# Attention, experts and MLP in one kernel on one core: another order for its first part

## The chip, the cores and the metric

The kernel runs on one core of a Trainium2 chip. The metric is the device time of one execution in microseconds (us). The time before is the median of three runs.

## The reference

What is computed, cut to what matters (B, H, S, D = 2, 8, 576, 64; 1152 tokens; all in float32):

```
scores = q @ k^T / sqrt(D) + cum[i] - cum[j]      # cum: running sum of log(clip(f, 1e-4, 1)); causal
attn   = softmax(scores);  x = attn @ v           # x: 1152 tokens x 512
p      = domain_probs / (domain_probs.sum(-1) + 1e-9)
y      = sum over 4 experts e of p[:, e] * (relu(x @ w1[e]) @ w2[e])     # 512 -> 1024 -> 512
out    = (h * sigmoid(1.702 h)) @ w_out,  h = y @ w_in                   # 512 -> 2048 -> 512
```

## The kernel before

**Tiles.** Tokens are the free dimension, in four chunks: chunk 0 is batch 0, tokens 0 to 255; chunk 1 batch 0, 256 to 575; chunks 2 and 3 the same of batch 1. Later, three wide chunks of 384 are used. Attention goes by units. A unit of chunk 0 (a "plain" unit) is one head and two tiles of 128 queries; a later unit is a pair of heads and one tile of 128 queries (64 of both heads in the last). A unit passes the stages of `STAGES` (L538): scores on TensorE into one of two `s` banks (L427), their maximum on VectorE (`mx`, L453), `exp` on ScalarE (L467), division by the sum on GpSimd (L478), transposes on TensorE (L497), one or two rounds of work later the product with the values (`x`, L527), and x split into a rounded part xh and a rest xl (L535).

**Split operands.** Weights and later keys and queries are written as a rounded part and a rest (`whi`, `wlo`; `khi`, `klo`; `qhi`, `qlo`), and a product is three matmuls instead of one. Weights come by DMA into four buffers `wst` of two groups each (`load_pair`), `whi` is made on ScalarE or GpSimd and `wlo` on VectorE (`split_w`, `split_rest`, L171). Keys and queries of a pair are split on GpSimd (`prep_parts`, `prep_queries`, L357 to L366), which also adds the causal mask to rows of `cum` broadcast from DRAM (`prep_cum`, `cb` and `cbs`, L379 to L388). Plain units take unsplit operands that were laid out on the host.

**Layers.** The experts and the MLP are cut into 12 blocks of 512 hidden columns (`NBLK`); a visit of a block computes its first layer (L619) for its chunks and its second layer (L663) for them, each as four groups g of 12 matmuls. Visit 0 is block 2 (expert 1) of chunk 0. Its first layer is not done at once but grows as heads of chunk 0 come out (`emit_first`, L640). `seq` (L126) is the order of layers: first layer of visit 0, first of visit 1, second of visit 0, first of visit 2, second of visit 1, and so on. The second layer's result is multiplied by the probabilities, broadcast over partitions as `dpb0` and `dpb1` (L674, L677), and summed in `acc`. `dpb0` and `dpb1` first hold the values of chunk 0, heads 0 to 3 and 4 to 7 (L310), and are loaded with probabilities of experts 0 and 1 from the DRAM tile `dpT` when those have been read (L776, L777); `dpT` is written from `dpn`, which `make_probabilities` makes on GpSimd and VectorE (L262 to L273). `ps_m` gives three banks for the layers' sums.

**Order.** All is written in program order in `attention()` (L545), one `yield` per unit, and in the main loop (L783), which pulls units between the layers' groups at a pace set by `due`. A scheduler then sets the order on each engine, except where `keep_in_program_order` pins an instruction. In the first loop (L761) each pull of chunk 0 is followed by dummy matmuls (`turn`, L712: `WARM` of them at the very start, then those of `FILL`) and, at pulls 4 to 7, by the split of the first weights `wa`. The preparation of a later pair of heads is made `LEAD` = 3 units ahead of its first unit; for the first pair that falls into chunk 0, behind the normalisation of one of its units (`pinned`, L561). The weights `wb` of visit 0 are split in the main loop, at the first group (L801).

## Time and profile before

| | us |
|---|---|
| median of 3 runs (lowest, highest) | 743.79 (742.61, 744.67) |
| the profiled execution, its own time | 741.27 |
| its span from first to last instruction | 739.6 |
| TensorE matmul busy (share of the span) | 717.7 (97%) |
| VectorE busy | 454.9 (62%) |
| GpSimd busy | 294.2 (40%) |
| ScalarE busy | 271.5 (37%) |
| mean granted clock of TensorE | 0.988 of 2.4 GHz |

The span lies inside the execution's own time. Matmuls are pipelined and overlap, so busy TensorE is not TensorE at its peak. PE is TensorE, DVE VectorE, ACT ScalarE, POOL GpSimd, SP SyncE, which issues most DMAs; an L number is a line of the kernel.

### The profile page before, as it was taken

The page shows a single profiled execution, that of the slowest core. Times are in us where ns is not written, and L with a number is a line of the kernel's source. Part 1 is how long each engine was busy: PE and PEld are TensorE (multiplying, and loading weights), DVE is VectorE, ACT ScalarE, POOL GpSimd, SP SyncE. Part 2 cuts the span into 40 slices and gives each one's busy share as a digit, 9 for nine tenths or more (in the row PEclk, how much of TensorE's full clock was granted, in tenths as well). Part 3 has the DMA queues.
Part 4 walks back from the last instruction along what each step waited for, and adds up shares of the span by engine and source line. Part 5 has one row for each costly group of instructions (what it writes and reads, how often), then busy time and mean ns, then how long its engine had stood idle before and what let it go on. Part 6 is the DMA issues. An engine that isn't in the chain of part 4 may idle for free.

```text
span 739.6 us, 12033 instructions
## 1 busy us (share of the span) xinstructions
PE 717.7 (97%) x4516; PEld 683.9 (92%) x4518; DVE 454.9 (62%) x1024; ACT 271.5 (37%) x634; POOL 294.2 (40%) x372
## 2 busy tenths in 40 slices
PE   7969799999999999999999999999999999999998
PEld 4757599899999999999999999999999999999997
DVE  4756455667757999999899733344973134334422
ACT  4565454556641233222212221222444433323420
POOL 3898776785333004223232433332452222222220
PEclk9998899999999999999999999999999999999999
DMA  8765643523216354553343301000100000000012
GB/s 285 241 191 168 207 157 101 168 81 97 75 48 226 132 188 158 174 177 121 120 145 105 102 2 56 1 1 1 58 0 1 1 1 1 1 1 0 1 43 86
DMA packets 31226, 68.83 MB, mean 93 GB/s; under 512 B 3224, under 2 KB 4768, under 8 KB 31168
## 3 DMA queue, kind: packets, MB, share of 16 engines
q1 hardware_dynamic: 31128, 68.02, 29.1%
q8 instruction: 36, 0.59, 0.3%
q14 instruction: 22, 0.18, 0.1%
q10 hardware_dynamic: 40, 0.04, 0.0%
HBM read 65.62 MB, written 2.41 MB: 92 GB/s over the span
## 4 chain that ended last, share of the span: by engine, by line
PE 88%; DMA 6%; DVE 5%; issue 1%; ACT 1%; SPq 0%; ACTq 0%; DVEq 0%
PE m L663 38%; PE m L619 37%; PE s L427 4%; PE x L527 4%; PE t L497 3%; DMA wst<-in_wa_moe_dram 1%; DVE wlo L171 1%; DMA mst<-in_wa_mlp_dram 1%; DMA dpT<-dpn 1%; DMA dpb<-dpT 1%; PE m L640 1%; DVE cvd L234 1%; PE m L712 1%; DMA kd<-fr 1%; DVE cvt L220 1%
## 5 line engine op out<-in xcount | busy, mean ns | idle before, releaser
L679 POOL TENSOR_TENSOR acc<-acc,tmp 128x384 f32<-128x384 f32 (+3 forms) x112 | 114.1, 1030 | 238.1 <-DVE tmp L677 237.7
L663 PE MATMUL m<-hh,whi 128*128 128x384 f32 (+2 forms) x640 | 128.7, 321 | 4.9 <-DVE acc L674 4.9
L663 PE MATMUL m<-hl,whi 128*128 128x384 f32 (+2 forms) x640 | 128.7, 320 | 0.0
L663 PE MATMUL m<-hh,wlo 128*128 128x384 f32 (+2 forms) x640 | 127.8, 320 | 0.8 <-DVE wlo L171 0.7
L619 PE MATMUL m<-xh,whi 128*128 128x384 f32 (+2 forms) x624 | 126.2, 322 | 0.0
L619 PE MATMUL m<-xh,wlo 128*128 128x384 f32 (+2 forms) x624 | 125.6, 321 | 0.0
L619 PE MATMUL m<-xl,whi 128*128 128x384 f32 (+2 forms) x624 | 124.7, 320 | 0.0
L56 ACT ACTIVATE whi<-wst 128x512 fp32r<-128x512 f32 x108 | 67.7, 631 | 126.6 <-PE m L619 72.2
L663 PEld LDWEIGHTS m<-hh,whi 128*128 128x128 f32 x640 | 106.1, 189 | 6.7 <-DVE acc L674 5.1
L663 PEld LDWEIGHTS m<-hh,wlo 128*128 128x128 f32 x640 | 106.2, 189 | 1.5 <-DVE wlo L171 1.4
L663 PEld LDWEIGHTS m<-hl,whi 128*128 128x128 f32 x640 | 106.8, 189 | 0.3
L619 PEld LDWEIGHTS m<-xh,whi 128*128 128x128 f32 x624 | 104.1, 189 | 0.6 <-DVE wlo L171 0.4
L619 PEld LDWEIGHTS m<-xh,wlo 128*128 128x128 f32 x624 | 104.2, 189 | 0.1
L619 PEld LDWEIGHTS m<-xl,whi 128*128 128x128 f32 x624 | 103.9, 189 | 0.1
L171 DVE TENSOR_TENSOR wlo<-wst,whi 128x512 fp32r<-128x512 f32 x112 | 89.8, 807 | 20.1 <-ACT whi L56 16.4
L654 POOL TENSOR_TENSOR hl<-tmp,hh 128x384 fp32r<-128x384 f32 x48 | 49.1, 1025 | 133.4 <-ACT hh L56 133.3
L645 ACT ACTIVATE hh<-m 128x384 fp32r<-128x384 f32 (+2 forms) x112 | 49.0, 438 | 117.6 <-PE m L619 117.2
L646 DVE SCALAR_TENSOR_TENSOR hl<-m,hh 128x384 fp32r<-128x384 f32 (+2 forms) x112 | 54.9, 495 | 34.6 <-ACT hh L645 34.4
L677 DVE TENSOR_TENSOR tmp<-m,dpb 128x384 f32<-128x384 f32 (+2 forms) x80 | 41.0, 513 | 31.8 <-PE m L663 28.5
L652 DVE TENSOR_TENSOR tmp<-m,sg 128x384 f32<-128x384 f32 x48 | 26.6, 554 | 54.2 <-ACT sg L651 54.2
L478 POOL TENSOR_SCALAR e<-e,sm 128x128 f32<-128x128 f32 (+4 forms) x72 | 47.1, 665 | 31.9 <-DVE sm L476 25.3
L467 ACT ACTIVATE e<-e,mx 128x128 f32<-128x128 f32 (+4 forms) x72 | 42.0, 584 | 33.1 <-DVE mx L453 28.2
(96 smaller groups left out, 772.5 us busy)
## 6 DMA issues: line engine op xcount, KB each, us to landing
wst<-in_wa_moe_dram SPq DMA_DIRECT2D x28, 512.0 KB, 4.1
wst<-in_wb_moe_dram SPq DMA_DIRECT2D x28, 512.0 KB, 3.7
mst<-in_wa_mlp_dram SPq DMA_DIRECT2D x16, 512.0 KB, 3.5
mst<-in_wb_mlp_dram SPq DMA_DIRECT2D x16, 512.0 KB, 4.6
cb<-cumd SPq DMA_DIRECT2D x16, 256.0 KB, 6.7
qr<-in_qk_dram SPq DMA_DIRECT2D x12, 256.0 KB, 6.8
kq<-in_qk_dram SPq DMA_DIRECT2D x8, 352.0 KB, 13.1
vd<-in_vp_dram SPq DMA_DIRECT2D x8, 320.0 KB, 4.4
```

The source lines that it names most:

```text
L56: return nc.scalar.activation(out=out, in_=in_, func=AF.Copy)
L171: sub = nc.vector.tensor_sub(lf, raw, f(hf))
L427: nc.tensor.matmul(pt[:, :z - a], lhsT=lr[i][0], rhs=lr[i][1], start=i == 0, stop=i == n - 1)
L467: nc.scalar.activation(out=e[:, off:off + w], in_=e[:, off:off + w], func=AF.Exp, scale=-1.0, bias=mx, accum_out=sm[:, 0, k:k + 1])
L478: last_norm[:] = [nc.gpsimd.tensor_scalar(out=e[:, off:off + w], in0=e[:, off:off + w], scalar1=sm[:, 0, i:i + 1], scalar2=1.0, op0=ALU.mu ...
L619: nc.tensor.matmul(p[:, :n], lhsT=w[:, k, :], rhs=x[c][:, k, :], start=(j == 0 and k == 0), stop=(j == 2 and k == 3))
L645: nc.scalar.activation(out=hh[:, g, :n], in_=p[:, :n], func=AF.Relu)
L646: nc.vector.scalar_tensor_tensor(out=hl[:, g, :n], in0=p[:, :n], scalar=0.0, in1=f(hh[:, g, :n]), op0=ALU.max, op1=ALU.subtract)
L654: nc.gpsimd.tensor_sub(hl[:, g, :n], t[:, :n], f(hh[:, g, :n]))
L663: nc.tensor.matmul(p[:, :n], lhsT=w[:, k, :], rhs=x[:, k, :n], start=(j == 0 and k == 0), stop=(j == 2 and k == 3))
L677: nc.vector.tensor_mul(t[:, :n], p[:, :n], d)
L679: nc.gpsimd.tensor_add(a, a, t[:, z])
```

## The change

- `make_probabilities` runs on VectorE and early, its input is loaded among the first DMAs, and `dpT` is written right behind the first four pairs of weights.
- Every load of the first part goes through `load`, which pins its place on SP's queue. Keys and queries of the first later pair come before the plain operands of heads 4 to 7 and before weights; the broadcasts of `cum` are loaded apart from the mask additions (`load_cum`).
- `prep_parts` and `prep_queries` of that first pair stand ahead of the first unit of chunk 0, and its maxima are pinned on VectorE. An empty unit is put in behind the plain units.
- `wa` of visit 0 is split at pulls 2 to 5, `wb` at pulls 7 to 10, with its rounded part on GpSimd.
- `seq` has the second layer of visit 0 right behind its first layer, and the last first-layer sum is evacuated at once.
- 14 dummy matmuls at the start instead of 12, 17 between the units instead of 18.

```diff
-WARM, FILL = 12, (4, 4, 3, 2, 1, 1, 1, 1, 1)
+WARM, FILL = 14, (4, 4, 3, 2, 1, 1, 1, 1)
+    def load(out, in_):
+        ins = nc.sync.dma_start(out=out, in_=in_)
+        if start[0]:
+            tc.keep_in_program_order(ins)
...
-    seq = [(1,) + units[0]]
-    for p_, u in zip(units, units[1:]):
+    seq = [(1,) + units[0], (2,) + units[0], (1,) + units[1]]
+    for p_, u in zip(units[1:], units[2:]):
...
+        hi_ins = (round_pool if v_ == 0 and kind == "b" or 0 < v_ <= 2 and g == 3 else round_act)(hf, raw)
...
-            if v_ == 0 and kind == "a":
+            if v_ == 0:
                 tc.keep_in_program_order(sub)
...
-        nc.gpsimd.tensor_add(s, v[:, 0], v[:, 1])
+        tc.keep_in_program_order(nc.vector.tensor_add(s, v[:, 0], v[:, 1]))
...
-        nc.gpsimd.tensor_mul(out, v, s.unsqueeze(1).to_broadcast([128, 4, NT // 128]))
-        nc.sync.dma_start(out=dpT.rearrange("e (p j) -> p e j", p=128), in_=out)
+        nc.vector.tensor_mul(out, v, s.unsqueeze(1).to_broadcast([128, 4, NT // 128]))
+        return out
...
+                if (c, u) == first_later:
+                    tc.keep_in_program_order(ins)
...
+    unit_seq.insert(max(i for i, (c, u) in enumerate(unit_seq) if plain(c)) + 1, (None, ((), ())))
...
+        prep_parts(*nxt[0])
+        prep_queries(*nxt[0], nxt[0][0][0][0])
...
+            if i == 0:
+                load_cum(*nxt[0])
+            if i == 4:
+                load_heads(*nxt[1])
...
     load_plain(0)
+    dp_raw = load_probabilities()
     load_plain(4)
...
             load_plain_rest(4)
+            load_heads(passes[1], 0, True)
             load_plain_late()
...
-    for _ in range(2):
-        load_pair(True)
-    load_heads(passes[1], 0)
+    dpn = make_probabilities(dp_raw)
+    for _ in range(4):
+        load_pair()
+    load(dpT.rearrange("e (p j) -> p e j", p=128), dpn)
+    load_values(passes[1], 0)
...
-        if pulled[0] in (4, 5, 6, 7):
-            split_w("a", 0, pulled[0] - 4)
-            split_rest()
+        for kind, p0 in (("a", 2), ("b", 7)):
+            if 0 <= pulled[0] - p0 < 4:
+                split_w(kind, 0, pulled[0] - p0)
+                split_rest()
...
-            if i == 0 and g == 0:
-                for k in range(4):
-                    split_w("b", 0, k)
+            if i == 0 and g == 3:
+                evac[0]()
+                evac[0] = lambda: None
```

The scheduler moves more than these lines say; three places in its order follow.

GpSimd, around the split of the first later pair (`kq` its keys, `qr` its queries; each pair of `e` rows is the normalisation of one unit of chunk 0, of which five stand ahead of this piece). Before:

```order
L478 TENSOR_SCALAR e<-e,sm 128x256
L53 TENSOR_SCALAR khi<-kq 128x704
L53 TENSOR_SCALAR qhi<-qr 128x256 x2
L357 TENSOR_TENSOR klo<-kq,khi 128x704
L366 TENSOR_TENSOR qlo<-qr,qhi 128x256 x2
L478 TENSOR_SCALAR e<-e,sm 128x128
```

With the change, from the last row of the setup on:

```order
L53 TENSOR_SCALAR tri<-ones 128x128
L53 TENSOR_SCALAR khi<-kq 128x704
L53 TENSOR_SCALAR qhi<-qr 128x256
L363 TENSOR_TENSOR klo<-kq,khi 128x704
L53 TENSOR_SCALAR qhi<-qr 128x256
L372 TENSOR_TENSOR qlo<-qr,qhi 128x256 x2
L491 TENSOR_SCALAR e<-e,sm 128x128
L491 TENSOR_SCALAR e<-e,sm 128x256
```

The split has moved from behind the fifth unit's normalisation to ahead of the first unit's.

TensorE, from the second pair's first scores on (L619 is a first layer, here that of visit 1). Before:

```order
L427 MATMUL s<-khi,qhi 128x384
L427 MATMUL s<-khi,qlo 128x384 x2
L427 MATMUL s<-klo,qhi 128x384 x2
L497 MATMUL t<-identr,e 128x128 x3
L619 MATMUL m<-xh,whi 128x256 x4
L497 MATMUL t<-identr,e 128x128 x3
```

With the change (L683 is the second layer, here of visit 0, and L639 the first):

```order
L683 MATMUL m<-hh,whi 128x256 x6
L683 MATMUL m<-hh,wlo 128x256 x4
L683 MATMUL m<-hl,whi 128x256 x3
L683 MATMUL m<-hh,whi 128x256
L683 MATMUL m<-hh,wlo 128x256 x4
L683 MATMUL m<-hl,whi 128x256 x5
L683 MATMUL m<-hh,whi 128x256 x4
L510 MATMUL t<-identr,e 128x128 x3
```

Behind the same scores now stand 27 matmuls of the second layer, and then the first transposes `t` of chunk 1 (pair 0, unit 0), where before they stood at once. Ahead of the last transposes of chunk 1 (pair 3, its third unit) the whole order has 235 matmuls of layers other than `emit_first`, where before it had 176.

SP's queue, around the two loads of broadcast probabilities (`dpb_76` is `dpb0`, `dpb_77` is `dpb1`). Before, with 46 rows ahead of the write of `dpT`:

```order
L273 DMA dpT<-dpn 128x4x9
L146 DMA wst<-in_wb_moe_dram 128x2x512
L385 DMA cbs<-cumd 128x1x576
L776 DMA dpb_76<-dpT 128x576
L777 DMA dpb_77<-dpT 128x576
```

With the change, where that write has 12 rows ahead of it:

```order
L796 DMA dpb_76<-dpT 128x576
L62 DMA wst<-in_wb_moe_dram 128x2x512
L62 DMA cb<-cumd 128x512 x2
L62 DMA cbs<-cumd 128x1x576
L62 DMA kq<-in_qk_dram 128x704
L62 DMA qr<-in_qk_dram 128x512
L62 DMA vd<-in_vp_dram 128x640
L797 DMA dpb_77<-dpT 128x576
```

`dpb1`, which the second layer of visit 0 needs first, is now loaded behind the rows of the second and third pair of chunk 1, in row 29 of the queue instead of row 51.

## Rows read from the trace of the kernel before

**Rows 1.** Page: TensorE's busy tenths and granted clock, 40 slices of the span.

```profile
PE   7969799999999999999999999999999999999998
PEclk9998899999999999999999999999999999999999
```

**Rows 2.** Windows: stretch and length; busy us by engine; PEclk; DMA share; GB/s.

```profile
0.00:9.10 9.10, 5.10 (x12) 1.67 (x13) 3.82 (x7) 3.60 (x5) 3.87 (x11) 1.00 0.74 175
9.10:27.86 18.76, 18.70 (x104) 12.89 (x106) 13.31 (x57) 11.78 (x43) 11.03 (x18) 0.91 0.88 320
27.86:66.50 38.64, 30.22 (x174) 22.09 (x174) 23.72 (x70) 19.69 (x53) 36.37 (x64) 0.91 0.65 202
66.50:100.00 33.50, 28.27 (x190) 24.54 (x189) 16.60 (x57) 16.78 (x45) 25.20 (x36) 0.90 0.53 159
100.00:739.60 639.60, 635.36 (x4044) 622.75 (x4043) 397.49 (x834) 219.63 (x491) 217.72 (x246) 1.00 0.24 75
```

**Rows 3.** Waits of TensorE: us in total, times, longest.

```profile
PE m L663 <- DVE acc L674: 4.9, 1, 4.9
PE s L427 <- DVE mx L453: 3.5, 2, 2.5
PE t L497 <- POOL e L478: 2.4, 3, 1.3
PE s L427 <- POOL qlo L366: 1.9, 1, 1.9
```

**Rows 4.** Timeline, TensorE: start, us, instruction, [idle before, releaser].

```profile
1.85 5.10 PE L712 MATMUL m<-acc 128*128 128x512 bf16 x12 [1.85 <-DVE acc L705]
...
27.86 0.51 PE L427 MATMUL s<-khi,qhi 128*128 128x384 f32 x2
...
50.16 0.64 PE L619 MATMUL m<-xh,wlo 128*128 128x256 f32 x4
50.64 0.64 PE L619 MATMUL m<-xl,whi 128*128 128x256 f32 x4
...
110.36 0.71 PE L497 MATMUL t<-identr,e 128*128 128x128 f32 x5
```

**Rows 5.** Timeline, GpSimd, in the same columns.

```profile
12.55 0.83 POOL L478 TENSOR_SCALAR e<-e,sm 128x128 f32<-128x128 f32 x2 [7.99 <-DVE sm L476]
...
16.67 1.26 POOL L478 TENSOR_SCALAR e<-e,sm 128x128 f32<-128x128 f32 x2 [0.98 <-ACT ph L56]
...
22.24 0.77 POOL L53 TENSOR_SCALAR khi<-kq 128x704 fp32r<-128x704 f32 x1
...
27.24 2.46 POOL L478 TENSOR_SCALAR e<-e,sm 128x128 f32<-128x128 f32 x6
...
41.38 3.05 POOL L478 TENSOR_SCALAR e<-e,sm 128x384 f32<-128x384 f32 x2
...
56.86 0.62 POOL L53 TENSOR_SCALAR whi<-wst 128x512 fp32r<-128x512 f32 x1
57.46 1.15 POOL L478 TENSOR_SCALAR e<-e,sm 128x384 f32<-128x384 f32 x2
```

**Rows 6.** Windows, GpSimd alone: all of a stretch; then instructions on `dps` alone.

```profile
29.67:105.40 75.73, 65.16 (x101) 0.91 0.60 185
...
40.00:80.00 40.00, 2.05 (x5) 0.91 0.62 187
```

**Rows 7.** Timeline, VectorE, in the columns of rows 4.

```profile
16.85 0.73 DVE L171 TENSOR_TENSOR wlo<-wst,whi 128x512 fp32r<-128x512 f32 x1
...
30.00 0.41 DVE L453 CUSTOM_DVE_ANT_0 e<-s,cb 128x256 f32<-128x256 f32 x1
...
39.77 4.28 DVE L171 TENSOR_TENSOR wlo<-wst,whi 128x512 fp32r<-128x512 f32 x5 [0.17 <-ACT whi L56]
```

**Rows 8.** Chain of waits that ended last: start, us, what.

```profile
4.49 4.48 DMA kd<-fr
...
75.43 6.76 DMA dpT<-dpn
82.60 6.65 DMA dpb<-dpT
```

More of the change, by code (lines that the diff above doesn't have):

```diff
@@ L145, in load_pair @@
             t = wst_p.tile([128, 2, 512], F32, tag="wst", name="wst")
[L146 to L148 removed]
+            load(t, (wa_moe if kind == "a" else wb_moe)[b, g:g + 2].rearrange("g p c -> p g c"))
             raw_w[kind, v_, g] = t[:, 0, :]
@@ L171, in rest @@
             sub = nc.vector.tensor_sub(lf, raw, f(hf))
-            if v_ == 0 and kind == "a":
+            if v_ == 0:
                 tc.keep_in_program_order(sub)
@@ L258, in load_probabilities @@
         raw = const.tile([128, NT // 32], F32, name="dpraw")
-        nc.sync.dma_start(out=raw, in_=dp)
+        load(raw, dp)
         return raw
@@ L310, in load_plain @@
         vd = (dpb1 if h0 else dpb0)[:, :2 * G * D].rearrange("p (t g d) -> p t g d", t=2, g=G)
-        for i, t in enumerate((kd, qd)):
-            if h0 == 0 or i == 0:
-                nc.sync.dma_start(out=t[0:64], in_=qk0[h0 // G, i].rearrange("d (g s) -> d g s", g=G))
+        if h0 == 0:
+            for i, t in enumerate((kd, qd)):
+                load(t[0:64], qk0[0, i].rearrange("d (g s) -> d g s", g=G))
         nc.gpsimd.memset(qd[64:65], 1.0 / NEG)
@@ L321, in load_plain_rest @@
         if h0 == 0:
-            tc.keep_in_program_order(nc.sync.dma_start(out=kd[64:65], in_=cum[h0:h0 + G, :wk]))
+            load(kd[64:65], cum[h0:h0 + G, :wk])
         else:
@@ L343, in load_heads, with load_values @@
         st["kq"] = kq_p.tile([128, KW], F32, tag="kq", name="kq")
-        nc.sync.dma_start(out=st["kq"], in_=src[:, :KW])
+        load(st["kq"], src[:, :KW])
         for i, c in enumerate(cs):
             st["q", c] = kq_p.tile([128, QW], F32, tag="qr", name="qr")
-            nc.sync.dma_start(out=st["q", c], in_=src[:, KW + i * QW:KW + i * QW + QW])
+            load(st["q", c], src[:, KW + i * QW:KW + i * QW + QW])
+        if not later:
+            load_values(p, h0)
+    def load_values(p, h0):
+        cs, b, s0 = p
+        st = pairs[p, h0]
         st["vd"] = v_p.tile([128, 5, 2, D], F32, tag="vd", name="vd")
-        nc.sync.dma_start(out=st["vd"], in_=vp[b * H // 2 + h0 // 2].rearrange("p (t g d) -> p t g d", t=5, g=2))
+        load(st["vd"], vp[b * H // 2 + h0 // 2].rearrange("p (t g d) -> p t g d", t=5, g=2))
     def prep_parts(p, h0):
@@ L366, in prep_queries, with load_cum @@
             nc.gpsimd.tensor_sub(lo[:, a:a + 256], raw[:, a:a + 256], f(hi[:, a:a + 256]))
+    def load_cum(p, h0):
+        cs, b, s0 = p
+        st = pairs[p, h0]
+        r = b * H + h0
+        st["cb"] = [cb_p.tile([128, 896], F32, tag="cb", name="cb") for _ in range(2)]
+        for g, cb in enumerate(st["cb"]):
+            load(cb[:, :512], cumd[r + g:r + g + 1, :512].to_broadcast([128, 512]))
+        st["cbs"] = cbs_p.tile([128, S], F32, tag="cbs", name="cbs")
+        load(st["cbs"], cumd[r:r + 2, :].unsqueeze(1).to_broadcast([2, 64, S]))
     def prep_cum(p, h0):
@@ L371, in prep_cum @@
         st = pairs[p, h0]
-        r = b * H + h0
-        st["cb"] = []
-        for g in range(2):
-            cb = cb_p.tile([128, 896], F32, tag="cb", name="cb")
-            nc.sync.dma_start(out=cb[:, :512], in_=cumd[r + g:r + g + 1, :512].to_broadcast([128, 512]))
+        for cb in st["cb"]:
             nb = (384 - s0) // 128
@@ L428, in emit_scores @@
         raw_s[c, u] = out
+    first_later = units_of(1, 0)[0]
     def emit_max(c, u):
@@ L566, in attention, with prepare @@
             done = None
-            new = [k for k in nxt if first[k] == i + LEAD]
-            new_q = [k for k, j in first_q.items() if j == i + LEAD]
-            if i > n0:
+            new = [k for k in nxt if first[k] == i + LEAD and k != nxt[0]]
+            new_q = [k for k, j in first_q.items() if j == i + LEAD and j > n0]
+            if i == 0:
+                load_cum(*nxt[0])
+            if i == 4:
+                load_heads(*nxt[1])
+            def prepare():
                 for k in new:
@@ L700, in attn_moe_mlp @@
     ones, mask = t[:16, :S], t[:, S:S + 256]
-    nc.sync.dma_start(out=fr, in_=fg)
+    load(fr, fg)
     nc.vector.memset(ones, 1.0)
```

58 lines of the change are left out of this document (20 added, 38 removed).

## Prediction, made before the result was seen

> **What bounds the kernel now.** I read the page's slices first. TensorE is busy nearly throughout, except in the first slice, the third and the fifth, and its granted clock is below full in the first five [rows 1]. A slice is 18.5 us, so whatever there is to gain lies in the first 100 us. The windows put sizes on it [rows 2]. From 100 us on TensorE is busy 635.36 of 639.60 us at full clock: there it is the bound, and an order of its work can give back 4.2 us at most, part of it the last store. From 27.86 to 66.50 us it is idle for 38.64 - 30.22 = 8.4 us, and a mean clock of 0.91, with only the levels 1.2 and 2.4 GHz, loses 38.64 x 0.09 = 3.5 us. From 66.50 to 100 us it is idle for 5.2 us and loses 33.5 x 0.10 = 3.35 us by the clock. Together that is 20.5 us. The waits tell who ends the idle times [rows 3]: 4.9 us in one piece is the second layer of visit 0, whose bank is not evacuated (`acc`, L674); the others come from the chain of attention, through maxima on VectorE and through GpSimd.
>
> Two chains stand behind this. The 4.9 us end with the load of broadcast probabilities: `dpT` is written at 75.43 us, takes 6.76 us, and the load behind it 6.65 us [rows 8]. So this wait hangs on when the probabilities are made, not on TensorE. The other is GpSimd: it splits the first later pair from 22.24 to 27.24 us, between two normalisations of chunk 0 [rows 5], is then at work for 65.16 of the 75.73 us up to the last normalisation of chunk 1 [rows 6], and does the first one of chunk 1 only at 41.38 us [rows 5].
>
> **The change part by part.**
>
> *Start.* The first scores wait for `kd<-fr`, issued at 4.49 and landed 4.48 us later [rows 8], behind five other loads, some 1.1 MB by their sizes. Now only some 0.55 MB stand ahead of it; landing in about half that time is 6.5 to 7 us. The 14 dummy matmuls take 14 x 5.10/12 = 5.95 us from 1.85 us on [rows 4], to 7.8 us, and these end last. The first scores start about 1.3 us earlier, against the 9.1 us where the first window was cut.
>
> *First chunk.* The split of 27.24 - 22.24 = 5.0 us [rows 5] leaves the stretch between the normalisations. Three costs come back. It now fills GpSimd from the landing of `kq`, about 8 us, to about 12.9 us, where the first normalisation stood at 12.55 us [rows 5]: 0.35 us. Two of four `wb` roundings, 0.62 us each [rows 5], stand ahead of the last normalisation: 1.2 us. VectorE gets two more `wlo` of 0.73 us [rows 7] before its first maximum of chunk 1. By GpSimd chunk 0 ends 5.0 - 0.35 - 1.2 = 3.4 us earlier; by VectorE, which has some 18.4 us of work between its first maximum, now near 8.7 us, and the first maximum of chunk 1 (30.00 us before [rows 7]), 2.9 us. I take 2.7 us, which contains the 1.3 us of the start; the ends are 1.0 and 4.7 us.
>
> Here the Trainium skill speaks against the change. Two normalisations that take 0.83 us took 1.26 us beside the `wlo` at 16.85 us, and two of 1.15 us took 3.05 us beside five of them at 39.77 us [rows 5, 7]. "SBUF — State Buffer", Who interferes with whom, says that a VectorE instruction with two SBUF inputs and a GpSimd instruction that reads SBUF exclude each other, and the rows agree. By it the extra `wlo` cost chunk 0 some 0.43 us each, and the 1.9 us at 41.38 us come back: the sum stays.
>
> The clock: TensorE ran its dummies to 6.95 us, idled to 9.10 us, and the next window has a mean clock of 0.91 [rows 2, 4], a loss of 18.76 x 0.09 = 1.7 us. Without the gap that may go. I count nothing for it, since VectorE and GpSimd set the pace of chunk 0. "TensorE: Matmul & The Clock Gate", The HAM clock gate, holds that the throttled clock is the default and that activity releases it; counted in full, that would make the sum 1.7 us lower.
>
> *Chunk 1, to 66.50 us.* The 8.4 us of idle time and 3.5 us of clock go if GpSimd is early enough: 11.9 us. In its queue from 29.67 us on, the five instructions on `dps` go, 2.05 us [rows 6], and two `wb` roundings come, 1.24 us. On VectorE the six small instructions that take their place stand between 6 and about 7.1 us, before the first maximum; the one measured neighbour in kind is the small work of rows 6, 0.41 us a piece, so 2.5 us at worst, then up to 8.5 us and still beside the first scores: nothing.
>
> *The probabilities, to 100 us.* `dpT` is written among the first loads, so the 4.9 us wait, the rest of 5.2 us and 3.35 us of clock go: 8.6 us. What replaces it: `dpb1` is now needed near 41 us instead of 85, by the bank of the fourth group of the early second layer. Its tile holds values until the last product of heads 4 to 7, which I put at 33 us; with 6.65 us [rows 8] it lands at about 40 us. That is just in time.
>
> *What comes back.* TensorE does 59 more matmuls of the layers before the last transposes of chunk 1 (235 against 176 in the order), 59 x 0.12 = 7.1 us (four take 50.64 - 50.16 = 0.48 us [rows 4]). With all the gains, 2.7 + 11.9 + 8.6 = 23.2 us, it reaches those transposes at 110.36 - 23.2 + 7.1 = 94.3 us. GpSimd without any idle time reaches its last normalisation of chunk 1 at 27.0 + 65.16 - 2.05 + 1.24 = 91.4 us. The margin is 2.9 us; GpSimd was idle 10.6 us there before [rows 6]. So it will hold TensorE up now and then. Between none and nine us I take 4.5 us.
>
> **Sum.** 741.27 - 23.2 + 4.5 = 722.6 us for an execution like the profiled one. The median of the three runs is 2.5 us above that one, so the forecast is 725 us.
>
> **Rivals.**
> 1. *GpSimd becomes the bound of chunk 1.* It repeats its 10.6 us of idle time, and chunk 0 gains only 1.0 us: its last normalisation of chunk 1 ends near 28.7 + 64.35 + 10.6 = 103.7 us and the transposes follow at 104 us. Gain 110.36 - 104 + 7.1 = 13.5 us, 728 us, with the 2.5 us 730 us. For it: GpSimd was at work for 36.37 of 38.64 us from 27.86 us on [rows 2]. Against: part of the idle time fell into the wait for the probabilities, which goes.
> 2. *`dpb1` comes late.* Its load stands on SP behind those of two more pairs. If it lands 5 us late, the old wait is back at 41 us instead of 85: 4.9 + 3.35 us, 733 us. Against: none of the loads just ahead of it needs a buffer that is still read, by the pools' counts (three for keys and queries, three for values, four for `cb`).
> 3. *Slower: VectorE and GpSimd in lockstep.* `wlo` of `wb` waits for a rounding on GpSimd that stands behind normalisations, and the maxima of chunk 1 stand behind that `wlo`. From 1.6 us a unit on over the 12 units of chunk 1 (18.7 us) nothing is left; at 2 us it is 725 + 24 = 749 us. For it: the five `wlo` at 39.77 us held maxima up [rows 7]. Against: only two of the four `wb` roundings stand behind the first scores of chunk 1, and each takes 0.62 us [rows 5].
> 4. *It does not do what it says:* the gaps move, and each us won is lost a little later: 743 us.
>
> **How the numbers follow.** Forecast 0.60, rival 1 0.18, rival 2 0.13, rival 3 0.05, rival 4 0.04. The range runs from 717 us (no hold-up, chunk 0 at its better end, 741.27 - 25.2 us, and 1.3 us to the lowest run) to 736 us (rival 2 and the worst of what comes back). It leaves out rivals 3 and 4 and the tails. A measurement can tell 0.3%, 2.2 us, from no change: faster is the forecast and rivals 1 and 2, 0.91; the same is rival 4, 0.04; slower 0.05.
>
> **What would show it.** Right: first scores near 7.8 us; the split of the first pair on GpSimd ahead of its first normalisation; the first scores of chunk 1 near 25 us instead of 27.86 us [rows 4]; the wait for `acc` gone; TensorE busy above 95% and at full clock from 30 to 100 us. Rival 1 would show as waits of `t` and of scores for GpSimd, rival 2 as one wait for `dpb<-dpT` near 41 us, rival 3 as VectorE waiting for `whi` on GpSimd. The prediction is wrong if the idle time and the low clock before 100 us stay above 12 us in all, or if new idle time shows behind 100 us, where I count on none.

## The result, and the profile after

Four runs of the changed kernel gave a median of 734.20 us (732.70 to 734.92), four of the kernel before 743.20 us (740.24 to 744.67). The ratio is 0.9881, with a 95% interval of 0.9845 to 0.9917: faster by 9.0 us. The forecast was 725 us, in a range of 717 to 736: the direction is right and the range holds the time, but of the 18.8 us forecast (743.79 - 725) less than half came. The profiled execution took 733.54 us, its span is 731.8 us.

The page's slices of the changed kernel, to be read beside [rows 1]:

```profile
PE   7987989999999999999999999999999999999998
PEclk9899999999999999999999999999999999999999
```

The clock's 8, in the fourth and fifth slice before, stands in the second alone now. The third and the fifth slice are fuller, 8 and 9 where they were 6 and 7, but the fourth is 7 now and the sixth 8, where both were 9: part of the idle time has only moved. The windows, with the cuts and columns of [rows 2], give sizes:

```profile
0.00:9.10 9.10, 7.25 (x27) 3.53 (x28) 5.47 (x19) 4.64 (x9) 5.26 (x13) 1.00 0.61 167
9.10:27.86 18.76, 15.99 (x76) 9.95 (x75) 10.37 (x45) 9.88 (x35) 9.77 (x18) 0.82 1.00 312
27.86:66.50 38.64, 31.81 (x207) 27.43 (x208) 24.07 (x74) 17.81 (x50) 33.07 (x57) 0.92 0.68 215
66.50:100.00 33.50, 30.63 (x236) 27.12 (x232) 22.86 (x67) 19.86 (x53) 25.72 (x34) 0.99 0.60 187
100.00:731.80 631.80, 625.45 (x3981) 614.73 (x3979) 397.73 (x826) 215.76 (x485) 217.12 (x252) 1.00 0.23 74
```

Idle time and clock loss together, worked out as in the prediction: from 9.10 to 27.86 us they grew from 1.7 to 2.8 + 3.4 = 6.2 us. From 27.86 to 66.50 us they fell from 11.9 to 6.8 + 3.1 = 9.9 us only. From 66.50 to 100 us they fell from 8.6 to 2.9 + 0.3 = 3.2 us. Behind 100 us there is 6.35 us of idle time where there was 4.24. So the last stretch, that of the probabilities, gave 5.4 us, the one ahead of it 2.0 us, and the second window lost 4.5 us.

The waits of TensorE up to 130 us, in the columns of [rows 3], say who ends the idle times now:

```profile
PE t L510 <- POOL e L491: 5.3, 4, 2.1
PE x L540 <- ACT ph L56: 4.5, 1, 4.5
PE s L436 <- DVE mx L464: 2.3, 4, 0.8
...
PE m L683 <- DVE acc L694: 0.2, 1, 0.2
```

The 4.9 us for `acc` are 0.2 us. In their place stands a wait of 4.5 us for `ph`, a copy on ScalarE that had not been on the list. The timelines of the engines show where both of the new losses come from. TensorE first:

```profile
1.85 5.04 PE L732 MATMUL m<-acc 128*128 128x512 bf16 x14 [1.85 <-DVE acc L725]
6.72 0.82 PE L436 MATMUL s<-kd,qd 65*128 65x128 f32 x4
...
13.25 0.33 PE L510 MATMUL t<-identr,e 128*128 128x128 f32 x1 [1.38 <-POOL e L491]
16.01 0.66 PE L510 MATMUL t<-identr,e 128*128 128x128 f32 x2 [1.24 <-ACT ph L56]
...
29.38 0.42 PE L436 MATMUL s<-khi,qhi 128*128 128x384 f32 x1
...
63.95 3.81 PE L540 MATMUL x<-ph,vd 128*64 128x320 f32 x16 [4.52 <-ACT ph L56]
```

and ScalarE:

```profile
14.07 1.15 ACT L56 ACTIVATE whi<-wst 128x512 fp32r<-128x512 f32 x2 [2.21 <-DMA wst<-in_wa_moe_dram]
...
62.24 0.63 ACT L56 ACTIVATE whi<-wst 128x512 fp32r<-128x512 f32 x1 [4.78 <-DMA wst<-in_wa_moe_dram]
```

The row at 29.38 us is the first scores of chunk 1. ScalarE works in order. Twice a rounding of `wa` stands at the head of its queue and waits for a load, with exponentials and `ph` copies behind it: 2.21 us at 14 us, 4.78 us at 62 us. After the first of these, with TensorE busy for 1.5 of the 4 us from 12 to 16 us, the granted clock is 0.50, the level of 1.2 GHz, from 16 to 22 us (the 0.82 of the second window). GpSimd has the same at 45.75 us:

```profile
8.16 0.78 POOL L53 TENSOR_SCALAR khi<-kq 128x704 fp32r<-128x704 f32 x1 [3.02 <-DMA kq<-in_qk_dram]
...
12.83 1.63 POOL L491 TENSOR_SCALAR e<-e,sm 128x128 f32<-128x128 f32 x4
...
45.75 0.70 POOL L397 TENSOR_TENSOR cbs<-cbs,tri 64x64 f32<-64x64 f32 x2 [3.25 <-DMA cbs<-cumd]
...
47.14 1.68 POOL L491 TENSOR_SCALAR e<-e,sm 128x384 f32<-128x384 f32 x2
```

The split of the first pair stands ahead of the first normalisation, as planned. But the first normalisation of chunk 1 comes at 47.14 us, where it came at 41.38 us [rows 5], because it stands behind sums with `cbs`, a load that lands late. The chain of waits that ended last, in the columns of [rows 8], names the loads:

```profile
8.25 5.79 DMA wst<-in_wa_moe_dram
...
33.34 12.34 DMA cbs<-cumd
...
50.43 11.70 DMA wst<-in_wa_moe_dram
```

### The profile page after: what moved, and what is told of

The parts are those of the page before. It is cut to its first block, busy times and chain, and to the rows that moved or that the text cites. A ratio compares the mean times of both kernels' runs of the same rounds, so it can differ in the third digit from the quotient of the medians.

```text
span 731.8 us, 12044 instructions
## 1 busy us (share of the span) xinstructions
PE 711.1 (97%) x4519; PEld 682.8 (93%) x4519; DVE 460.5 (63%) x1029; ACT 267.9 (37%) x630; POOL 291.0 (40%) x371
## 4 chain that ended last, share of the span: by engine, by line
PE 69%; DVE 14%; DMA 6%; POOL 5%; issue 3%; ACT 1%; SPq 1%; DVEq 0%; ACTq 0%; POOLq 0%
PE m L683 32%; PE m L639 30%; PE s L436 3%; PE x L540 3%; DVE wlo L173 3%; DMA wst<-in_wa_moe_dram 2%; PE t L510 2%; DMA cbs<-cumd 2%; POOL e L491 2%; DVE cvd L236 1%; DVE hl L666 1%; DVE tmp L697 1%; DVE wf L230 1%; DVE cvt L224 1%; DMA mst<-in_wb_mlp_dram 1%
## 5 line engine op out<-in xcount | busy, mean ns | idle before, releaser
L699 POOL TENSOR_TENSOR acc<-acc,tmp 128x384 f32<-128x384 f32 (+3 forms) x112 | 111.7, 1009 | 237.3 <-DVE tmp L697 235.3
L683 PE MATMUL m<-hh,whi 128*128 128x384 f32 (+2 forms) x640 | 129.3, 321 | 0.2 <-DVE acc L694 0.2
L683 PE MATMUL m<-hh,wlo 128*128 128x384 f32 (+2 forms) x640 | 127.7, 320 | 1.2 <-DVE wlo L173 1.2
L683 PE MATMUL m<-hl,whi 128*128 128x384 f32 (+2 forms) x640 | 128.0, 319 | 0.0
L639 PE MATMUL m<-xh,wlo 128*128 128x384 f32 (+2 forms) x624 | 126.3, 320 | 0.0
L639 PE MATMUL m<-xl,whi 128*128 128x384 f32 (+2 forms) x624 | 126.2, 321 | 0.0
L639 PE MATMUL m<-xh,whi 128*128 128x384 f32 (+2 forms) x624 | 125.6, 321 | 0.0
L56 ACT ACTIVATE whi<-wst 128x512 fp32r<-128x512 f32 x104 | 65.3, 632 | 128.9 <-PE m L639 69.0
L173 DVE TENSOR_TENSOR wlo<-wst,whi 128x512 fp32r<-128x512 f32 x112 | 92.7, 830 | 24.6 <-ACT whi L56 18.2
L683 PEld LDWEIGHTS m<-hh,wlo 128*128 128x128 f32 x640 | 106.2, 189 | 1.9 <-DVE wlo L173 1.9
L683 PEld LDWEIGHTS m<-hh,whi 128*128 128x128 f32 x640 | 106.8, 190 | 0.6 <-DVE acc L694 0.4
L683 PEld LDWEIGHTS m<-hl,whi 128*128 128x128 f32 x640 | 106.4, 188 | 0.2
L639 PEld LDWEIGHTS m<-xh,wlo 128*128 128x128 f32 x624 | 104.1, 188 | 0.2
L639 PEld LDWEIGHTS m<-xl,whi 128*128 128x128 f32 x624 | 104.0, 188 | 0.2
L639 PEld LDWEIGHTS m<-xh,whi 128*128 128x128 f32 x624 | 103.7, 188 | 0.2
```

What stands on the lines that cost most here:

```text
L56: return nc.scalar.activation(out=out, in_=in_, func=AF.Copy)
L173: sub = nc.vector.tensor_sub(lf, raw, f(hf))
L639: nc.tensor.matmul(p[:, :n], lhsT=w[:, k, :], rhs=x[c][:, k, :], start=(j == 0 and k == 0), stop=(j == 2 and k == 3))
L683: nc.tensor.matmul(p[:, :n], lhsT=w[:, k, :], rhs=x[:, k, :n], start=(j == 0 and k == 0), stop=(j == 2 and k == 3))
L699: nc.gpsimd.tensor_add(a, a, t[:, z])
```

## The experiments

Eighteen kernels were timed, each beside the kernel before, whose median was between 741.6 and 743.6 us from one group of them to the next; between groups the ratios tell more than the medians. The order of the instructions comes from a scheduler that plans with modelled durations, so an edit moves more than its own lines; differences of less than about 0.3% between two of these kernels are not read. The ratios are to the kernel before, with 95% intervals.

| kernel | us | ratio | interval |
|---|---|---|---|
| the change | 734.20 | 0.9881 | 0.9845 to 0.9917 |
| probabilities alone (e6) | 734.18 | 0.9886 | 0.9857 to 0.9914 |
| `wa` split late (e2) | 731.15 | 0.9848 | 0.9823 to 0.9874 |
| `cb`, `cbs` of pair 2 early (e1) | 737.59 | 0.9931 | 0.9905 to 0.9957 |
| both (e3) | 731.51 | 0.9856 | 0.9832 to 0.9881 |
| e2 with the first pair inside chunk 0 (e5) | 733.65 | 0.9875 | 0.9853 to 0.9896 |
| e2 with normalisation first (e7) | 733.07 | 0.9866 | 0.9845 to 0.9888 |
| e2 with the old order of layers (e8) | 732.44 | 0.9859 | 0.9837 to 0.9882 |
| e2 with heads unpinned (e9) | 738.46 | 0.9944 | 0.9923 to 0.9965 |
| e2 with 2.8 MB fewer loads (e10) | 734.12 | 0.9886 | 0.9866 to 0.9907 |
| e2 with 9.3 us less GpSimd work (e11) | 736.18 | 0.9911 | 0.9891 to 0.9931 |
| e2 with `cb`, `cbs` on ScalarE's queue (e12) | 734.87 | 0.9898 | 0.9879 to 0.9917 |
| e2 with weights on ScalarE's queue (e13) | 737.90 | 0.9933 | 0.9913 to 0.9953 |
| the change, `cbs` in two loads (e14) | 726.69 | 0.9752 | 0.9728 to 0.9776 |
| e2 and `cbs` in two loads (e15) | 720.10 | 0.9678 | 0.9657 to 0.9699 |
| before, `cbs` in two loads (e16) | 734.51 | 0.9867 | 0.9841 to 0.9892 |
| e7 and `cbs` in two loads (e17) | 720.90 | 0.9695 | 0.9669 to 0.9721 |
| e15 with the first pair inside chunk 0 (e19) | 720.09 | 0.9714 | 0.9700 to 0.9727 |
| e15 with the old order of layers (e20) | 718.55 | 0.9697 | 0.9679 to 0.9715 |

### The parts of the change, one at a time

**e6**, the kernel before with the probabilities made early on VectorE:

```diff
-        nc.gpsimd.tensor_add(s, v[:, 0], v[:, 1])
+        tc.keep_in_program_order(nc.vector.tensor_add(s, v[:, 0], v[:, 1]))
...
+    tc.keep_in_program_order(nc.sync.dma_start(out=dpT.rearrange("e (p j) -> p e j", p=128), in_=dpn))
```

> The kernel before with one part of the change alone: the probabilities are made on VectorE behind the cumulative sums, and dpT is written behind the first weight loads. The forecast's term for this part (4.9 us of wait for acc, 0.3 us of other idle time and 3.35 us of clock) gives 743.2 - 8.6 = 734.6 us if nothing comes back. Rival (the wait covered a late GpSimd: once it is gone TensorE meets the chain of attention instead): 738 to 741 us, with the idle time of 75 to 90 us gone and new waits for e or ph up to 110 us.

A ratio of 0.9886 is some 8 us less, so this part alone gives as much as the whole change. That it is close to the term of 8.6 us is partly chance, as its windows show:

```profile
0.00:9.10 9.10, 6.35 (x23) 2.86 (x24) 5.71 (x17) 4.48 (x9) 3.87 (x11) 1.00 0.67 152
9.10:27.86 18.76, 18.76 (x117) 13.15 (x116) 14.22 (x62) 11.69 (x44) 14.49 (x26) 1.00 0.90 311
27.86:66.50 38.64, 28.67 (x169) 23.27 (x169) 21.60 (x60) 19.30 (x50) 31.68 (x52) 0.82 0.74 235
66.50:100.00 33.50, 31.86 (x254) 28.88 (x252) 24.08 (x77) 22.36 (x59) 24.90 (x36) 1.00 0.65 193
```

In the stretch of the term, from 66.50 us on, idle time and clock loss fall from 8.6 to 1.6 us, so the term itself gives 7.0 us. From 27.86 to 66.50 us they grow from 11.9 to 16.9 us. And the scheduler also put the load of `kq` behind `kd<-fr`, so the first scores came at 7.27 us instead of 9.10, and the second window runs at full clock: that takes idle time and clock loss in the first two windows from 5.7 to 2.8 us.

**e2**, the splits of `wa` later, and **e1**, the broadcast loads of the second pair earlier; **e3** is both:

```diff
-        for kind, p0 in (("a", 2), ("b", 7)):
+        for kind, p0 in (("a", 5), ("b", 7)):
```

> Edit to the changed kernel: the four splits of wa of visit 0 stand in steps 5 to 8 of the attention instead of 2 to 5. Theory S (ScalarE, which works in order, stands 2.2 us before the exponentials of the second pair for a weight load that lands at 14.04 us, and TensorE idles and falls to half clock behind it): that wait goes, TensorE stays at full clock up to 28 us, and the first scores of chunk 1 come near 26 us instead of 29.38. By theory Q the end of chunk 1 is set by cbs, so the time falls by 1 us at most, to 733 to 734. Rival: the chain of chunk 0 is as long without that wait (scores of chunk 1 still above 28.5 us), 734; a gain of 3 us in the time would say that Q is wrong.

```diff
             if i == 4:
                 load_heads(*nxt[1])
+                load_cum(*nxt[1])
```

> Edit to the changed kernel: the broadcast loads of the second later pair (two cb, one cbs) are issued right behind its keys, queries and values, instead of behind the wb loads that wait for a buffer. Theory Q (the load queue stands behind a pinned load that waits, from 20.5 to 31.9 us, and the burst behind it makes cbs land 12.3 us after its issue): cbs lands before 33 us instead of 45.68, the first normalisation of chunk 1 moves from 47.14 to about 42 us, the 3.25 us wait of GpSimd goes, and the time falls by 3 to 5 us, to about 730. Rival G (GpSimd's own work sets the end of chunk 1): the wait goes but the normalisations come no earlier by more than 1 us, 734. Rival B (the transfers share one rate, and what is moved ahead makes others late): cbs is early, a weight load is late in its place, 733 to 736.

> Both edits, the splits of wa in steps 5 to 8 and the broadcast loads of the second pair early. By S and Q together the two add: first scores of chunk 1 near 26 us, its first normalisation near 39 us, and 727 to 728 us. If GpSimd's own work sets the end of chunk 1: 731 or more.

With the late splits ScalarE's wait at 14 us is gone, the first scores of chunk 1 come at 25.23 us instead of 29.38, and the second window runs at full clock:

```profile
25.23 0.34 PE L436 MATMUL s<-khi,qhi 128*128 128x384 f32 x1
```

```profile
9.10:27.86 18.76, 17.84 (x104) 12.07 (x104) 14.30 (x58) 11.14 (x42) 12.59 (x24) 1.00 1.03 319
27.86:66.50 38.64, 30.60 (x205) 24.97 (x204) 23.49 (x70) 17.91 (x47) 33.24 (x54) 0.96 0.74 226
```

Theory S holds. But of the 4.1 us won there the time shows 3 us or less: TensorE is idle for 8.0 us from 27.86 to 66.50 us. Theory Q falls with e1: the load of `cbs` was issued at 22.46 us, eleven microseconds earlier, and landed only at 40.6. GpSimd's wait for it fell from 3.25 to 0.35 us, but the rests `klo` and `qlo` of the second pair stood ahead of the first normalisation of chunk 1, which moved from 47.14 to 46.26 us only, and the time grew, with chunk 0 late as well (first scores of chunk 1 at 30.74 us). e3, which mends that, is no better than e2.

**e5** undoes the split of the first pair ahead of chunk 0 in e2, **e8** the second layer at once:

```diff
-        prep_parts(*nxt[0])
-        prep_queries(*nxt[0], nxt[0][0][0][0])
...
+                        if i == n0 - LEAD:
+                            prep_parts(*nxt[0])
+                            prep_queries(*nxt[0], nxt[0][0][0][0])
```

> The kernel with the late splits of wa, and of the change one more part undone: the first later pair is split by GpSimd in the middle of chunk 0, behind the normalisations of its fifth and sixth heads, as it was before. The forecast's step (the 5.0 us of that split stand in the way of chunk 0, and moving it ahead brings 1 to 4.7 us): chunk 0, from its first scores to the first scores of chunk 1, gets 2.5 to 4 us longer than the 17.6 us of the run with the late splits, and the time is 733.5 to 735. Rival (VectorE, TensorE and ScalarE set the pace of chunk 0; GpSimd has slack there, as the run with the probabilities alone suggests, with 17.1 us and the split in the middle): 17.0 to 18.2 us, and the time 730.5 to 732.

```diff
-    seq = [(1,) + units[0], (2,) + units[0], (1,) + units[1]]
-    for p_, u in zip(units[1:], units[2:]):
+    seq = [(1,) + units[0]]
+    for p_, u in zip(units, units[1:]):
...
-            if i == 0 and g == 3:
-                evac[0]()
-                evac[0] = lambda: None
```

> The kernel with the late splits of wa, and the second layer of visit 0 behind the first layer of visit 1 again, as before the change. If the second layer at once is worth something (work for TensorE while chunk 1 waits): 732 to 735. If it is neutral: 730.5 to 732. If it costs (it needs wb and dpb while the transfers are behind): 728 to 730.

In e5 chunk 0 lasts from 7.60 to 24.19 us, 16.6 us, a microsecond shorter than with the split ahead (7.63 to 25.23). So GpSimd's split does not stand in the way of chunk 0 in these kernels. The time of e5, 733.65 us, lies where the forecast's step had it, but chunk 0 is no longer for it, and the times of e2, e5 and e8 can't be told apart. e19 and e20 ask the same two questions again where the loads are no longer in the way (below).

### What holds chunk 1 up

**e7** puts the sums of the second pair behind the first normalisation of chunk 1:

```diff
                     load_cum(*k)
-                    prep_cum(*k)
+                    if i > n0:
+                        prep_cum(*k)
...
+                    if k == "norm" and i == n0 + 1:
+                        with pinned(last_norm):
+                            prep_cum(*nxt[1])
```

> The kernel with the late splits of wa, and on GpSimd the sums of the second later pair (cb, cbs with tri, which wait 3.5 us for the load of cbs) behind the first normalisation of chunk 1 instead of ahead of it. Theory N (the first normalisation of chunk 1 stands behind that wait in GpSimd's queue, so what chunk 0 wins is lost there): the first normalisation comes at 36 to 38 us instead of 44.44, the 2.0 us wait of TensorE for e goes with most of the idle time of 35 to 45 us, and the time is 727 to 729. Rival D (transfers: the loads of weights and of cbs land no earlier, and the units behind wait for them instead): the normalisation is early, the idle time moves to the second pair or to the wait for ph near 60 us, and the time stays 730 to 732.

The normalisation came at 37.00 us, 7.4 us earlier than in e2, and the time did not fall: TensorE waited 2.9 us for `ph` at 62 us and 3.3 us for `e` at 78 us instead. Rival D, as far as this goes.

**e9** delays the heads of the third to fifth pair by two steps, which puts them out of the pinned order; the scheduler then issued them at once, ahead of the weights of visit 1:

```diff
-                    load_heads(*nxt[n])
+                    heads_due.append((i + 2 if n in (2, 3, 4) else i, nxt[n]))
+            while heads_due and heads_due[0][0] <= i:
+                load_heads(*heads_due.pop(0)[1])
```

> The kernel with the late splits of wa, and the keys, queries and values of the third and fourth later pair no longer pinned behind the loads that wait for a buffer: they stand ahead of the weights of visit 1, in the stretch in which the queue stood. Theory D (the transfers of 28 to 55 us are one burst, each load takes 12 us in it, and ScalarE's 5.6 us wait for a weight near 59 us is its end): the burst is shorter by 1.8 MB at 300 GB/s, about 4 us, ScalarE's wait near 59 us falls below 3 us, and the time to 727 to 729. Rival N (GpSimd's queue sets the pace): the first normalisation of chunk 1 stays at 43 to 45 us and the time at 730 to 732. If the weights of visit 1 become late instead (they now stand behind 1.5 MB): a wait for whi near 35 us and 733 or more.

Worse: GpSimd starts on `cbs` of the second pair at 48.5 us, and ScalarE's wait for a weight near 60 us grew from 5.6 to 6.4 us. Filling the hole in the queue with other loads cost more than it gave.

**e10** takes loads away, **e11** work of GpSimd. e10 leaves out the loads of keys, queries and values of heads 2 to 7 for chunk 1, whose units then work on those of heads 0 and 1, so its output is another; e11 leaves out the low parts of keys and queries of the same heads and takes those of heads 0 and 1 for them:

```diff
+        if p == passes[1] and h0:
+            st.update({k: pairs[p, 0][k] for k in ("kq", ("q", 1), "vd")})
+            return
```

> The kernel with the late splits of wa; it leaves out the loads of the keys, queries and values of heads 2 to 7 for chunk 1, whose units work on those of heads 0 and 1, so the attention output of these heads is that of others; all work of the engines stays. 2.8 MB of some 14 MB go from the loads of 15 to 45 us. Theory D (transfers set the pace of chunk 1): cbs of the second pair lands 4 us earlier or more, ScalarE's 5.6 us wait for a weight near 59 us falls below 2 us, and the time falls by 5 us or more, to 726 or less. Theory G (GpSimd's own work sets it): the waits shrink but the normalisations of the later units do not move by more than 2 us, 729 to 731.

```diff
+        if p == passes[1] and h0:
+            st["lo"] = pairs[p, 0]["lo"]
+            return
...
+            if not same:
+                nc.gpsimd.tensor_sub(lo[:, a:a + 256], raw[:, a:a + 256], f(hi[:, a:a + 256]))
```

> The kernel with the late splits of wa; it leaves out the low parts of keys and queries (klo, qlo) of heads 2 to 7 for chunk 1, whose products use those of heads 0 and 1, so their scores are less exact; 3 x (1.7 + 1.4) = 9.3 us of GpSimd's work go, all loads stay. Theory G: the last normalisation of chunk 1 (107.2 us) comes 5 us earlier or more, and the time falls to 726 or less. Theory D: GpSimd waits longer for cbs and ScalarE for weights, the wait near 59 us stays at 4 us or more, and the time is 729 to 731.

Neither gained; e11 is some 5 us slower than e2, for a reason that is open. That was the turning point: with 2.8 MB less to load GpSimd starts on the second pair's `cbs` 13.8 us after its issue and on the third pair's 15.3 us after, and ScalarE still waits 5.4 us for a weight. GpSimd's timeline in e10 (the third pair) and ScalarE's:

```profile
55.00 0.70 POOL L400 TENSOR_TENSOR cbs<-cbs,tri 64x64 f32<-64x64 f32 x2 [4.45 <-DMA cbs<-cumd]
```

```profile
56.01 0.63 ACT L56 ACTIVATE whi<-wst 128x512 fp32r<-128x512 f32 x1 [5.44 <-DMA wst<-in_wa_moe_dram]
```

and with GpSimd relieved it waits all the longer, 5.22 us, for the same load, which lands at the same 43 us as in e2:

```profile
43.29 0.70 POOL L405 TENSOR_TENSOR cbs<-cbs,tri 64x64 f32<-64x64 f32 x2 [5.22 <-DMA cbs<-cumd]
```

**e12** and **e13** give part of the loads to ScalarE's queue:

```diff
-            load(cb[:, :512], cumd[r + g:r + g + 1, :512].to_broadcast([128, 512]))
+            (load if p == passes[1] and h0 < 4 else nc.scalar.dma_start)(out=cb[:, :512], in_=cumd[r + g:r + g + 1, :512].to_broadcast([128, 512]))
...
```

> The kernel with the late splits of wa, and the broadcast loads of the third and all later pairs (two cb, one cbs each) issued from ScalarE's queue instead of SyncE's. Theory H (the order in one queue: a load that waits holds up the ones behind it, and no more than eight are under way): with two queues the weights and cbs are issued earlier, GpSimd's waits for cbs at 77 and 93 us (5.6 and 3.3 us) fall below 2 us, and the time to 727 to 729. Theory D (rate of the transfers): the waits stay, 730 to 732. If the issues on ScalarE hold up its exponentials: 733 or more.

```diff
-            load(t, (wa_moe if kind == "a" else wb_moe)[b, g:g + 2].rearrange("g p c -> p g c"))
+            (load if w_loaded[0] <= 6 else nc.scalar.dma_start)(out=t, in_=(wa_moe if kind == "a" else wb_moe)[b, g:g + 2].rearrange("g p c -> p g c"))
```

> The kernel with the late splits of wa, and the weights from the second layer of visit 1 on issued from ScalarE's queue instead of SyncE's. Theory H: the loads of wa of visit 2 are issued near 40 us instead of 46.85, land near 50, and ScalarE's 5.6 us wait near 59 us goes: 727 to 729. Theory D: they are issued earlier and land no earlier than 57 us, or cbs lands later in their place, 730 to 733.

Both are slower than e2, and GpSimd starts on `cbs` of the second pair, which stays on SyncE's queue, at 43.28 and 42.77 us again. e12 does not test the order of the queue cleanly, since ScalarE itself stands for 4.83 us until 44.49 us. Still, neither the amount (e10), nor the order in the queue (e1), nor GpSimd's work (e11) is what makes the load late: in e2, e11, e12 and e13 one load lands at 43 us, 13.5 to 13.8 us after its issue.

### One load on two of sixteen DMA engines

What the load itself does is seen where little else is under way. Windows of the changed kernel, in the columns of [rows 2], at places near the landing of a `cbs`:

```profile
44.50:45.50 1.00, 1.00 (x6) 1.00 (x5) 0.94 (x5) 0.38 (x1) 0.00 (x0) 0.50 0.14 54
45.50:46.50 1.00, 1.00 (x7) 1.00 (x6) 0.00 (x0) 0.00 (x0) 0.63 (x2) 0.50 0.12 49
94.00:95.00 1.00, 1.00 (x8) 0.91 (x7) 0.55 (x2) 0.42 (x1) 0.32 (x1) 1.00 0.13 51
108.00:109.00 1.00, 1.00 (x11) 1.00 (x10) 0.53 (x1) 0.00 (x0) 1.00 (x2) 1.00 0.13 51
```

The mean share of the 16 DMA engines is 0.13, which is two engines, and they move 51 GB/s, where full windows move 300 to 400. The packets in the trace agree. From 108 to 109 us all that move data have 2304 bytes, one row of `cbs`. From 44.3 to 46.4 us two packets are under way at a time, and rows of 2304 bytes are mixed with rows of 2048, 2560 (as `vd` has) and 2816 bytes (as `kq` has): the rest of other loads, on the same two engines. The kernel before has such places too:

```profile
24.00:25.00 1.00, 1.00 (x10) 0.68 (x9) 0.68 (x2) 0.45 (x3) 1.00 (x2) 1.00 0.13 51
...
36.00:37.00 1.00, 1.00 (x9) 0.55 (x7) 1.00 (x4) 0.00 (x0) 0.63 (x2) 1.00 0.13 51
...
53.00:54.00 1.00, 0.84 (x7) 0.64 (x5) 0.00 (x0) 1.00 (x3) 1.00 (x2) 1.00 0.14 53
```

`cbs` is loaded in one piece from 2 rows, each to 64 partitions: its outermost dimension is 2. At 51 GB/s its 288 KB take 5.8 us alone, an estimate, and two such loads, or other loads' shares on those two engines, queue behind each other, as the mixed rows above show. The Trainium skill says this of a load's shape: "DMA: Bandwidth & Descriptors", Rules for kernel authors, has it that a small outermost dimension confines the whole load to at most as many engines, and asks for a multiple of 16 there. The trace agrees: 0.13 x 16 = 2.1 engines. The edit, in the changed kernel (**e14**), in e2 (**e15**), in the kernel before (**e16**) and in e7 (**e17**):

```diff
-        load(st["cbs"], cumd[r:r + 2, :].unsqueeze(1).to_broadcast([2, 64, S]))
+        for g in range(2):
+            load(st["cbs"][64 * g:64 * g + 64], cumd[r + g:r + g + 1, :].to_broadcast([64, S]))
```

> The changed kernel with one edit: cbs of a pair comes by two loads of 64 partitions, one row each, instead of one load whose outermost dimension is the 2 rows. Theory K (the one load runs on 2 of 16 DMA engines, at 51 GB/s: 288 KB take 5.8 us alone and more behind others, and every load that waits for it, by the limit of loads under way or by GpSimd's order, is late): no stretch with a share of 0.13 is left, cbs of the second pair lands within 7 us of its issue, before 41 us instead of 45.7, GpSimd's waits for cbs (3.25, 5.17, 2.30 us) shrink below 1 us each, and the time falls by 3 to 6 us, to 728 to 731. Rival (general shortage, or the next wait takes over): 733 to 735.

> Both: cbs in two loads, and the splits of wa of visit 0 late. Theory K: the two add, 725 to 728, with the first normalisation of chunk 1 before 40 us (44.44 with the late splits alone). Rival: 730 to 732, as with the late splits alone.

> The kernel before with cbs in two loads alone. Theory K: cbs of the second pair, issued near 19 us, no longer lands at 36.2 us but before 30; the first normalisation of chunk 1 (41.38 us) comes 2 us earlier or more; but the 4.9 us wait for the probabilities stays, so the time falls by 1 to 4 us only, to 739 to 742. Rival: within 1 us of the kernel before.

> cbs in two loads, the late splits of wa, and the sums of the second pair behind the first normalisation of chunk 1. With cbs early the order on GpSimd should matter less: theory K 724 to 728, equal to the kernel without the last edit within 1.5 us; if GpSimd's order is then what is left, 1.5 us or more below that one.

All four gained more than theory K had them gain. The work and the bytes are unchanged, and the changed kernel goes from 734.2 to 726.7 us, with the late splits from 731.2 to 720.1, and e7 from 733.1 to 720.9 (in ratios 0.9881 to 0.9752, 0.9848 to 0.9678, 0.9866 to 0.9695). The kernel before falls to 734.5 us, by 9.1 us where 1 to 4 were expected: this load had cost it as much as the whole change brings. In e14 chunk 0 is still late (first scores of chunk 1 at 31.24 us), which the late splits mend in e15 (25.28 us). The first normalisation of chunk 1 is hardly earlier in e14 (46.49 us), yet idle time and clock loss from 27.86 to 66.50 us fall from 9.9 to 4.1 us: the loads behind matter more than this one moment. The instructions that touch `cbs` in e15, in the view of one tile:

```profile
  DMA cbs<-cumd: 0.4, 1
...
DMA to landing us min/median/max: 3.5/5.2/7.7
```

GpSimd waits 0.4 us for it up to 130 us (10.9 us in the changed kernel), and it lands in 5.2 us at the median. The windows of e15:

```profile
9.10:27.86 18.76, 17.05 (x103) 12.07 (x103) 12.94 (x58) 11.22 (x42) 12.74 (x24) 1.00 1.04 332
27.86:66.50 38.64, 35.98 (x263) 31.30 (x263) 28.02 (x87) 23.69 (x62) 38.14 (x61) 1.00 0.80 265
66.50:100.00 33.50, 31.59 (x248) 28.13 (x247) 22.73 (x71) 19.53 (x56) 33.04 (x47) 1.00 0.64 191
100.00:718.50 618.50, 613.65 (x3889) 603.67 (x3887) 391.14 (x799) 209.61 (x466) 204.10 (x231) 1.00 0.23 72
```

TensorE is idle for 2.7 us from 27.86 to 66.50 us and never at its lower clock; GpSimd is at work for 38.14 of 38.64 us and 33.04 of 33.50 us. That suggests that GpSimd sets the pace there now, as the first rival had it for the kernel as changed; no run takes work from it here. ScalarE's wait for a weight near 60 us is gone too, though nothing was done to that load.

How a late `cbs` holds up other loads was seen, not tried: in e2 SyncE issues it at 29.45 us, seven more loads up to 36.76 us, and the next one at 43.04 us, in the moment in which GpSimd starts on the landed `cbs`. In e8 and e11 it is again seven more, and the next at 42.73 and 43.29 us, with GpSimd at 42.74 and 43.29; the load that had to wait is one of `kq` in e2 and e8 and one of `cb` in e11, which speaks against a buffer as the cause. I read that as eight loads under way at most.

**e19** and **e20** undo the two remaining parts in e15, by the edits of e5 and e8:

> The kernel with cbs in two loads and late splits of wa (720.1 us), with the first later pair split in the middle of chunk 0 again. If GpSimd's 5.0 us stood in the way of chunk 0, as the forecast held: first scores of chunk 1 at 28 us or later instead of 25.28, and 722.5 to 725. If GpSimd has slack in chunk 0: first scores of chunk 1 between 24 and 26 us, and 719 to 721.5.

> The same kernel with the second layer of visit 0 behind the first layer of visit 1 again. If the second layer at once is worth work for TensorE while chunk 1 waits: 722 to 725. If it is neutral: 719 to 721.5.

Neither is told apart from e15: 720.09 and 718.55 us beside 720.10. By the ratios e19 is some 2.7 us behind e15, with intervals that just fail to overlap, so a small worth of the early split is not excluded. In e19 chunk 0 lasts from 7.02 to 23.79 us, with the split in its middle. e15, e17, e19 and e20 all beat both kernels by 12 us or more; which of them is best is not told apart.

## Why the prediction was right and wrong

**Start: right in kind.** The first scores came at 6.72 us; I had put 7.8. The 14 dummies took 5.04 us, not 5.95; in the runs with the same 14 they took 4.5 to 6.1 us, and the first scores came at 6.3 to 7.8 us, so one row [rows 4] was too little to price them.

**First chunk: wrong, in its sign and in its reason.** The forecast has the first scores of chunk 1 near 25 us; they came at 29.38. I had costed the early splits of `wa` by VectorE's and ScalarE's time for them and not asked when their load lands: 14.04 us, at the head of an in-order queue. e2 takes that away and comes to 25.23 us, the forecast's number, but for another reason than the forecast's: that the split of 5.0 us leaves the stretch brought no shorter chunk 0 (e5, e19). For the clock I had counted nothing "since VectorE and GpSimd set the pace of chunk 0". Chunk 0 lasts 18.8 us at 0.91 before [rows 2, 4], and at 1.00 it lasts 17.6 us in e2 and 16.6 us in e5, but 18.5 us in e7, which starts a microsecond earlier than e2 and comes to 25.14 us all the same. So an earlier start is not carried to the end of chunk 0, and what the clock is worth there no run shows by itself. Beside its sum the prediction had set what the Trainium skill says in "TensorE: Matmul & The Clock Gate", The HAM clock gate: the throttled clock is the default, and activity releases it. The rows agree with that: where the gap of 2.15 us between the dummies and the first scores is gone (e2, e7) or is 0.9 us (e6), the stretch runs at 1.00.

**Chunk 1, to 66.50 us: the step that failed.** "The 8.4 us of idle time and 3.5 us of clock go if GpSimd is early enough": 11.9 us counted, 2.0 us won. GpSimd was early with its split, and in e11 another 9.3 us of its work went, and it made no difference, because the work behind was waiting for `cbs`, and the loads behind `cbs` for their turn (e14, e15). With `cbs` in two loads and the late splits the same window loses 2.7 us instead of 11.9: the term is 9.2 us then. I had read the rows of the waits, which name GpSimd and VectorE, and not followed GpSimd's own waits to the loads; the DMA share of 0.65 in [rows 2] looked like room to spare, and part of it is two engines at work and fourteen idle.

**Probabilities: right, and somewhat smaller.** The wait for `acc` is 0.2 us, and `dpb1` was in time. Where the sum has 8.6 us, the stretch from 66.50 to 100 us gives 5.4 us in the changed kernel, 7.0 in e6 and 6.7 in e15. The six small instructions on VectorE stand between 6.29 and 7.60 us, and the first maximum comes 0.80 us after the first scores, where it came 0.61 us after: they cost 0.2 us at most.

**What comes back: sized for the wrong place.** I had 4.5 us for GpSimd. Behind 100 us the changed kernel has 2.1 us more idle time than before, e15 0.6 us. The prediction's own test, "wrong if the idle time and the low clock before 100 us stay above 12 us", is met: they are 14.3 + 6.8 = 21.1 us in the changed kernel, and 8.1 + 0 us in e15. Its second test, new idle time behind 100 us, is met by the 2.1 us.

**Rivals.** None of the four had the load of `cbs`. The second had a late load, but that of `dpb1`, which was in time; it dismissed the loads with "none of the loads just ahead of it needs a buffer that is still read", which asks about buffers and not about how long a load takes. What e1, e7, e10 and e11 show is the fourth, each us won is lost a little later, confined to chunk 1; the time fell between that rival's 743 us and the forecast, near the second's 733, whose mechanism did not occur. That the range holds 734.2 us is therefore luck: its upper part stands on that second rival. (Its end of 736 us does not come out of its own terms either: 733 and the worst of what comes back, 9 instead of 4.5 us, make 737.7.)

The windows account for 3.0 of the 7.8 us by which the span fell; the rest lies in TensorE's busy time, whose ends are modelled. Counted by work, TensorE is busy behind 100 us for 9.9 us less than before (625.45 against 635.36), and the 2.1 us of new idle time take from that. So the gain was made ahead of 100 us, but 4.8 us of it show as no idle time and no clock loss there, and stay open.

## What to carry to other kernels

An idle time is won only up to the next thing that its releaser waits for: follow the releaser's own waits until they end at an engine that works or at a load, and for a load ask how many DMA engines carry it. A DMA share near 2/16 at a moment in which somebody waits for a load was the sign here that a load with an outermost dimension of 2 stood in the queue; two loads with 64 partitions each cost one more issue and were worth 7 to 12 us. On an in-order engine, an instruction that waits for a load belongs behind the work that others wait for, however short it is.
